# A convolution over windows of three token quarters, and copies that two engines share, in a fused convolution and wave-MLP kernel

## The chip, the cores and the metric

The kernel runs on one core of a Trainium2 chip. The metric is the device time of one execution in microseconds (us), the median of several runs. The engines are named as in the profile: PE is TensorE (matmul; PEld are its weight loads), DVE is VectorE, ACT is ScalarE, POOL is GpSimd, SP is SyncE. SP computes nothing; it issues DMA transfers. PSUM, where matmuls write, has eight banks.

## The reference

With x of shape 8 x 4224 x 192 (batch, tokens, channels), the reference computes a causal convolution over tokens with 7 taps, whose weights are a softmax per head (8 heads of 24 channels), and then a wave-MLP layer on its result:

```
w   = softmax(weight)                         # 8 heads x 7 taps
x   = sum_k w[h, k] * x_padded[b, s + k, h]   # 6 zero tokens ahead
theta  = x @ w_theta                          # 192 x 192
zr, zi = x * cos(theta), x * sin(theta)
y   = w_tok_r @ zr + w_tok_i @ zi             # 4224 x 4224, over tokens
u   = x + y
out = u + relu(u @ w_ch)                      # 192 x 192
```

Nearly all the arithmetic is in the two products over tokens. They have the form of a block product of two-by-two blocks.

## The kernel before

**Tiles.** Batch and channels together are 1536 columns (N), taken in two halves of 768 (HN), each worked on as two groups of 384 (PC, index g). The 4224 input tokens are 33 chunks of 128; a chunk c is not 128 neighbouring tokens but four quarters of 32, one from each fourth of the sequence (`tokens(c, a)` with a = 0 to 3). So a quarter of chunk c+1 follows directly on the same quarter of chunk c. The output tokens are units of two blocks of 128.

**A chunk's way** (class `Chunk`). POOL loads the four quarters of x, which casts them to bf16 (`load_x`, L224), into a tile `xw` of 96 partitions with two halves; in each half stand two quarters of 32 tokens with 16 history rows ahead of each. The history rows are copied from the previous chunk's tile by four DMAs on SP (`history`, L265). Convolution (`conv`, L403): for each head two matmuls of 192 columns, one per half, accumulate into a PSUM bank; the stationary operand `bands` holds the taps as a banded matrix. Two heads share a bank, so a chunk takes four banks and four copies of 384 columns on ACT to the tile `xz` (`conv_copy`, L411). From `xz` go: DMAs to a scratch in DRAM (`xs`, L298), used later as residual; a transposition into `uT`, by PE (L438) and a DVE copy (L443) for the first 11 chunks, by DMA later; the product with theta's weights (L452), copied and clamped by DVE into `ang` (L320); sine and cosine by ACT (L348); products with `xz` by DVE (L357); and three or four differences by DVE (L369), of which `t4` is the last. The product over tokens takes seven block products in place of eight, which is why the differences of blocks are needed.

**Visits.** The kernel has 11 slots for finished chunks. A visit takes one output unit and multiplies it with all chunks that lie in slots (L659); chunk c enters at visit c for the first 11 and one by one later, so the first visits are short: v+1 chunks at visit v, with 14 matmuls of 384 columns per chunk. A visit's token weights are loaded by POOL (8 DMAs, tiles `st`, L485), turned by DVE (L507) and combined by DVE (L521). Its six PSUM banks (rows x, y and s, two groups each) are added to accumulators `d`: the first sum on ACT (L684), later ones on DVE (L686); after the first product one bank is copied to another on ACT (L731). Accumulators are stored to and loaded from DRAM between visits (`part`, L698 and L621). After a unit's last visit `output` casts u to bf16 (ACT, L780), turns it (DMA, or PE for the last four visits), multiplies it with `w_ch` (L452), applies relu and adds (DVE, L799), and stores (L806).

**Order.** The program writes every engine's order out itself. All work is a list of `Step`s with an engine, a supposed duration, what must come before, and a due time; `Schedule` plays the list through with these supposed durations, first as a rehearsal, and issues the instructions of each engine in the order that results. Engines then execute in that order. Six PSUM banks belong to the visits; two (numbers 6 and 7, `mm`) are for convolution, transposition and channel products, and a step that reads such a bank frees it (`frees`). `Ring`s count the buffers of `xw`, `xz`, `uT`, `ang` and others, two of each. `START` gives the times from which engines take part, after what is issued before the list: ahead of it stand the first loads of x, the masks (POOL), the bands (DVE) and 18 matmuls on zeros (L881).

Of the kernel before, what the change touches and what calls it, by code (L numbers as in the profile page):

```python
# [10 lines left out]
ALU = mybir.AluOpType  # L11
# [5 lines left out]
def kernel(  # L17
# [32 lines left out]
    HALO = 16  # L50
    WR = Q + HALO
    NT = S // P
    HN = N // 2
# [7 lines left out]
    BY_PE = 4  # L61
    SMALL = 3
# [77 lines left out]
    def pair(u):  # L140
        return 2 * u + 1 < NT


# [22 lines left out]
    class Step:  # L166
        def __init__(self, engine, us, run, after=(), lands=0.0, wire=0.0, frees=None, mm=False):
            self.engine, self.us, self.run = engine, us, run
            self.after, self.lands, self.wire = list(after), lands, wire
            self.frees, self.mm = frees, mm  # L170
            self.due, self.want, self.fixed, self.end = None, None, None, None
            self.number = len(steps)
            steps.append(self)

# [20 lines left out]

    bands = constp.tile([2 * WR, 2 * H + 1, 2, Q], BF16, name="bands")
    nc.vector.memset(bands, 0.0)


    def channel_weights(w, name, after=()):  # L200
# [3 lines left out]
        def clear():  # L204
            made["t"] = t = wk.tile([P, 4, D], BF16, name=name, tag="wc", bufs=1)
            dve(nc.vector.memset(t[:, 1:3, :], 0.0))

        ready = [Step("dve", 0.25, clear, after)]
        for lo, hi, k, r0, r1 in ((0, P, 0, 0, P), (0, R, 1, P, D), (R, P, 2, 0, R), (0, P, 3, R, D)):
            ready.append(Step(  # L210
                "pool", 0.6, lambda lo=lo, hi=hi, k=k, r0=r0, r1=r1: pool(nc.gpsimd.dma_start(
                    out=made["t"][lo:hi, k, :], in_=w[r0:r1, :]
                )), ready[:1], lands=4.0, wire=0.3,
            ))
        return (lambda: made["t"]), ready

    xw = tiles(wk, 2, [2 * WR, 2, B, D], BF16, "xw")
    rings = {k: Ring(2) for k in ("xw", "xz", "uT", "ang", "xr", "st", "x", "y", "s")}
# [4 lines left out]
    def load_x(c, a, n, lo, t0, h, k):  # L223
        pool(nc.gpsimd.dma_start(  # L224
            out=xw[k][lo : lo + n, h, :, :],
            in_=x[:, t0 : t0 + n, :].rearrange("b s d -> s b d"),
        ))


    class Chunk:  # L230
        def __init__(self, c):
            self.c, self.early = c, c < SLOTS
            self.k, self.uses, prev = rings["xw"].take()
            self.loads = []
            for a in range(NQ):
                h, lo = a // 2, (a % 2) * WR
                t0 = tokens(c, a)
                if c or t0 == 0:
                    lo += HALO
                else:  # L240
                    t0 -= HALO
                n = (a % 2 + 1) * WR - lo
                args = (c, a, n, lo, t0, h, self.k)
                if c == 0:
                    if t0 == 0:
                        nc.vector.memset(xw[0][0:HALO, 0, :, :], 0.0)
                    load_x(*args)
                    s = Step("none", 0.0, None)
                    s.fixed = START["x0"]
                else:  # L250
                    s = Step(
                        "pool", 0.6, lambda args=args: load_x(*args), [prev],
                        lands=LAND["x"], wire=0.87,
                    )
                self.loads.append(s)
            self.uses += self.loads
            chunks[c] = self
            xwk = xw[self.k]
            self.filled = list(self.loads)
            if c:  # L260
                before = chunks[c - 1]

                def history(a):
                    h, lo = a // 2, (a % 2) * WR
                    sp(nc.sync.dma_start(  # L265
                        out=xwk[lo : lo + HALO, h, :, :],
                        in_=xw[before.k][lo + Q : lo + Q + HALO, h, :, :],
                    ))

                for a in range(NQ):  # L270
                    s = Step(
                        "sp", 0.6, lambda a=a: history(a), [before.loads, prev],
                        lands=LAND["history"], wire=0.15,
                    )
                    before.uses.append(s)
                    self.filled.append(s)
            self.uses += self.filled[NQ:]

        def prepare(self):
            c = self.c  # L280
            zk, self.xzuse, prev = rings["xz"].take()
            self.xz = xzt[zk]
            copies = []
            for hp in range(H // 2):
                m = Step("pe", 0.34, lambda b, hp=hp: self.conv(b, hp), [self.filled, bands_ready, prev], mm=True)
                self.uses.append(m)
                e = Step(
                    "act", 0.5, lambda b, hp=hp: self.conv_copy(b, hp), [m], frees=m
                )
                copies.append(e)  # L290
            self.xzuse += copies
            self.xf = self.xz[:, :, :].rearrange("p b d -> p (b d)")
            if c + 2 < NCH:
                Chunk(c + 2)
# [8 lines left out]
            for g in range(2):  # L303
# [3 lines left out]
                turned = transposed(src, uT, [copies, prev], self.early, "sp")  # L307
# [757 lines left out]
```

## Time and profile before

| | before |
|---|---|
| median of 3 runs, us | 1449.01 (1439.24 to 1450.27) |
| profiled execution, us | 1439.62 |
| its span, us | 1437.5 |
| mean granted TensorE clock | 0.997 |
| PE, DVE, ACT, POOL busy | 98%, 77%, 23%, 36% |
| matmuls: products over tokens / channel products / convolution / turns / on zeros | 7656 / 1056 / 528 / 228 / 18 |

The span reaches from the first to the last instruction; the profiled execution's own time is 2.1 us longer. In a line of the page's groups stand: line of the kernel, engine, operation, what is written and read, shape, number, then busy us in total, mean ns of one, and the engine's idle time just before these instructions with what ended it. In the timeline stand the start, the length from first start to last end, and what a stretch of equal instructions was. Matmuls overlap one another, so the mean length of one is not its cost. The chain of work that ended last is followed back from the last instruction; its shares say who set the time.

### The profile page before, as it was taken

The numbers are of one execution on the slowest core, as the hardware profiler recorded it, in microseconds if no ns is written. First come the engines' busy times: TensorE is split into PE (matmuls) and PEld (weight loads), VectorE is DVE, ScalarE is ACT, GpSimd is POOL, SyncE is SP. The second block draws the span as 40 slices with busy tenths as digits, with TensorE's granted clock in tenths as the row PEclk, the third lists the DMA queues.
The fourth block names the chain that finished last, engine by engine and source line by source line (L and its number), as shares of the span: only waits on it lengthen the run. The fifth ranks groups of instructions, "written<-read, shape, count | busy, mean of one in ns | idle before, by whom it ended". The sixth has DMA issues, their size and how long they took to land.

```text
span 1437.5 us, 24960 instructions
## 1 busy us (share of the span) xinstructions
PE 1408.2 (98%) x9486; PEld 895.5 (62%) x9486; DVE 1102.9 (77%) x1835; ACT 335.8 (23%) x582; POOL 512.2 (36%) x778
## 2 busy tenths in 40 slices
PE   6899999999999999999999999999999999999997
PEld 3666666666666666666666666666666666666665
DVE  7998764446778887886576788788887878787788
ACT  5764422122212212210000221122121212121221
POOL 7543321124234552133134445225553354311120
PEclk9999999999999999999999999999999999999999
DMA  9999883679999999998799999999995999999984
GB/s 140 252 220 209 155 162 94 122 131 238 202 222 239 237 225 229 225 210 198 183 195 193 234 252 234 220 224 217 250 253 124 204 279 257 220 229 208 254 209 154
DMA packets 341351, 298.44 MB, mean 208 GB/s; under 512 B 160784, under 2 KB 287760, under 8 KB 341232
## 3 DMA queue, kind: packets, MB, share of 16 engines
q0 software_dynamic: 171072, 97.81, 50.5%
q1 hardware_dynamic: 130160, 189.21, 42.6%
q10 hardware_dynamic: 40000, 9.84, 5.3%
q8 instruction: 74, 1.21, 0.4%
q14 instruction: 45, 0.37, 0.1%
HBM read 250.21 MB, written 106.56 MB: 248 GB/s over the span
## 4 chain that ended last, share of the span: by engine, by line
PE 90%; DMA 4%; DVE 2%; ACT 1%; issue 0%; ACTq 0%; DVEq 0%
PE bank L659 82%; PE bank L452 5%; DMA ubT<-ubT 3%; PE bank L403 3%; DMA out_dram<-d 1%; PE bank L438 1%; DVE d L799 0%; DVE d L686 0%; DVE w L521 0%; DMA xw<-xw 0%; DVE ubT L443 0%; ACT ubT L780 0%; DVE uT L443 0%; ACT bank L731 0%; DVE ang L320 0%
## 5 line engine op out<-in xcount | busy, mean ns | idle before, releaser
L659 PEld LDWEIGHTS <-w 128*128 128x128 bf16 x7572 | 736.7, 98 | 466.5 <-issue 5.1
L659 PE MATMUL bank<-t,w 128*128 128x384 bf16 x3198 | 558.4, 326 | 1.6 <-DVE w L521 1.4
L686 DVE TENSOR_TENSOR d<-bank,d 128x384 f32<-128x384 f32 x542 | 291.8, 548 | 186.0 <-PE bank L659 158.0
L659 PE MATMUL bank<-i,w 128*128 128x384 bf16 x2220 | 396.2, 326 | 1.2 <-ACT bank L731 0.6
L507 DVE STREAM_TRANSPOSE w<-st 128x640 bf16<-128x640 bf16 (+5 forms) x416 | 340.2, 846 | 67.0 <-PE bank L659 63.0
L659 PE MATMUL bank<-r,w 128*128 128x384 bf16 x2154 | 384.1, 326 | 1.4 <-DVE r L357 1.2
L485 POOL DMA_DIRECT2D st<-in_moe_w_tok_r_dram x244 | 140.2, 585 | 411.4 <-DVE w L507 354.5
L485 POOL DMA_DIRECT2D st<-in_moe_w_tok_i_dram x244 | 139.8, 583 | 145.8 <-DVE w L507 138.8
L521 DVE TENSOR_TENSOR w<-w 128x1408 bf16<-128x1408 bf16 (+10 forms) x220 | 183.2, 833 | 2.5
L631 POOL TENSOR_TENSOR d<-d,xr 128x768 f32<-128x768 f32 x62 | 105.6, 1704 | 142.1 <-DMA xr<-xs 91.8
L224 POOL DMA_DIRECT2D xw<-in_x_dram x132 | 76.8, 594 | 153.6 <-PE bank L403 128.0
L348 ACT ACTIVATE r<-ang,half_pi 128x768 bf16<-128x768 f32 x44 | 41.1, 933 | 310.3 <-DVE ang L320 310.3
L731 ACT ACTIVATE bank<-bank 128x384 f32<-128x384 f32 x116 | 54.8, 476 | 211.8 <-PE bank L659 196.7
L684 ACT ACTIVATE d<-bank 128x384 f32<-128x384 f32 x132 | 63.4, 491 | 160.4 <-PE bank L659 158.8
L411 ACT ACTIVATE xz<-bank 128x384 bf16<-128x384 f32 x132 | 60.5, 489 | 168.8 <-issue 115.4
L320 DVE TENSOR_SCALAR ang<-bank 128x384 f32<-128x384 f32 x132 | 68.5, 550 | 24.8 <-PE bank L452 24.4
L780 ACT ACTIVATE ubT<-d 128x768 bf16<-128x768 f32 x44 | 36.8, 842 | 147.1 <-DVE d L686 116.3
L799 DVE SCALAR_TENSOR_TENSOR d<-bank,d 128x384 f32<-128x384 f32 x106 | 55.3, 550 | 20.7 <-PE bank L452 20.1
L452 PEld LDWEIGHTS <-uT 128*128 128x128 bf16 x632 | 55.0, 98 | 17.0 <-issue 3.0
L403 PE MATMUL bank<-xw,bands 96*128 96x192 bf16 x528 | 60.6, 249 | 1.9 <-ACT xz L411 1.1
L452 PE MATMUL bank<-wth,uT 128*128 128x192 bf16 x528 | 58.0, 246 | 2.6 <-DVE ang L320 1.1
L403 PEld LDWEIGHTS <-bands 96*128 96x128 bf16 x528 | 47.4, 99 | 15.3 <-issue 4.0
(68 smaller groups left out, 546.3 us busy)
## 6 DMA issues: line engine op xcount, KB each, us to landing
part<-d SPq DMA_DIRECT2D x172, 384.0 KB, 4.2
d<-part SPq DMA_DIRECT2D x159, 384.0 KB, 5.5
st<-in_moe_w_tok_r_dram POOLq DMA_DIRECT2D x152, 176.0 KB, 6.5
st<-in_moe_w_tok_i_dram POOLq DMA_DIRECT2D x152, 176.0 KB, 7.4
out_dram<-d SPq DMA_DIRECT2D x53, 384.0 KB, 5.8
xs<-xz SPq DMA_DIRECT2D x132, 96.0 KB, 5.0
xr<-xs POOLq DMA_DIRECT2D x66, 192.0 KB, 6.4
xw<-in_x_dram POOLq DMA_DIRECT2D x129, 96.0 KB, 5.7
```

The lines of the kernel that those rows point to most:

```text
L224: pool(nc.gpsimd.dma_start(out=xw[k][lo : lo + n, h, :, :], in_=x[:, t0 : t0 + n, :].rearrange("b s d -> s b d"),))
L320: "dve", 0.55, lambda b, k2=k2, g=g: dve(nc.vector.tensor_scalar(out=self.ang[g][:, k2 * 2 * D : (k2 + 1) * 2 * D], in0=banks[b][:, 0 : 2 ...
L403: pe(nc.tensor.matmul(banks[b][:, hh * B * G : (hh + 1) * B * G], lhsT=bands[:, at : at + 2, :, :].rearrange("p z a m -> p (z a m)"), rhs= ...
L411: act(nc.scalar.activation(out=self.xz[:, :, hp * 2 * G : (hp + 1) * 2 * G].rearrange("p b (h g) -> p h b g", h=2), in_=banks[b][:, 0 : 2 ...
L452: pe(nc.tensor.matmul(banks[bk][:, b * D : (b + 1) * D], lhsT=tT[:, 3 * k + b + i, :], rhs=w[:, 2 * b + i, :], start=(i == 0), stop=(i == ...
L485: "pool", 0.58, lambda a=a, t0=t0, i=i, w=w: pool(nc.gpsimd.dma_start(out=st[i][a * Q : (a + 1) * Q, 0:nb, 0 : n * Q], in_=w[r0 : r0 + nb ...
L507: lambda c=c, ce=ce: dve(nc.vector.transpose(self.tile(name)[:, c:ce, :, :], st[i][:, at : at + NQ, c * Q : ce * Q].rearrange("p bt (c j) ...
L521: s = Step("dve", 0.15 + 0.069 * n, lambda: dve(nc.vector.tensor_tensor(out=flat(self.tile(name)), in0=flat(self.tile(p)), in1=flat(self.t ...
L631: a = Step("pool", 1.75, lambda: pool(nc.gpsimd.tensor_tensor(out=tile_(), in0=tile_(), in1=xrt[k], op=ALU.add)), [r, s])
L659: pe(nc.tensor.matmul(banks[bank][:, 0:PC], lhsT=self.w.block(a, c), rhs=chunks[c].operand(b, g), start=(start and c == self.lo), stop=(c ...
L684: act(nc.scalar.activation(out=o, in_=y, func=AT.Copy))
L686: dve(nc.vector.tensor_tensor(out=o, in0=y, in1=o, op=ALU.add))
```

## The change

The convolution no longer works on chunks but on windows. All quarters of all chunks in one row (chunk 0's four, chunk 1's four, and so on) are taken three at a time: 44 windows. A window's tile has 114 partitions: three times 32 tokens with their own 6 halo rows, loaded from DRAM together. So there are no copies of history, one matmul per head (`bands` has the taps of three quarters side by side and a zero block; which 128 columns are used depends on where the window's first quarter lies in its chunk), and a window's rows belong to one chunk or two. Its banks are copied in one or two pieces, each a range of partitions that starts at 0, 32, 64 or 96.

`copy_step` makes copies that may run on ACT or DVE: the planner puts a step with `also` into both engines' lists, and whichever is free first in its play takes it. That holds for the convolution copies of the first four chunks, the first sums and bank copies of the first four visits, and all copies of PE transposes.

In the beginning four banks of the first visit (2 to 5) are lent (`lent`) to the convolutions of the first two windows and to the transposes and theta products of the first chunk; two matmuls clear banks of the first visit afterwards. Windows 0 and 1 and theta's weights are loaded ahead of the list, before any token weights. The bands are made by one multiply for all taps and a tree of adds. The matmuls on zeros are 24, and their weights are zeros too, so they wait for DVE's memset and not for POOL's identity. `xw` and `xz` have three buffers each; the late tiles that took their space are split between both.

```diff
+    WQ = 3
+    ROWS = Q + KS - 1
+    WR = WQ * ROWS
...
+    EITHER, TURNED = 4, 11
...
+    def copy_step(o, i, after, us, frees=None, either=False):
+        def run(*b):
+            if s.engine == "dve":
+                dve(nc.vector.tensor_copy(out=o(), in_=i(*b)))
+            else:
+                act(nc.scalar.activation(out=o(), in_=i(*b), func=AT.Copy))
+        s = Step("act", us, run, after, frees=frees)
+        s.also = "dve" if either else None
+        return s
...
+    class Window:
+        def __init__(self):
...
+            self.k, self.uses, prev = rings["xw"].take()
+            for j in range(WQ):
+                c, a = divmod(self.m * WQ + j, NQ)
+                lo, t0, n = j * ROWS, tokens(c, a) - KS + 1, ROWS
...
+                    s = Step("pool", 0.6, load, [prev], lands=LAND["x"], wire=1.0)
+        def conv(self):
...
+                if lo % 2 and hi - lo > 1:
+                    copies.append((c, lo, lo + 1))
+                    lo += 1
+                copies.append((c, lo, hi))
+            at = -a0 % NQ
+            def conv(b, hp):
+                for hh in range(2):
+                    h = 2 * hp + hh
+                    pe(nc.tensor.matmul(
+                        banks[b][:, hh * B * G : (hh + 1) * B * G],
+                        lhsT=bands[:, h, at : at + NQ, :].rearrange("p z m -> p (z m)"),
+                        rhs=xw[self.k][0:WR, :, h * G : (h + 1) * G],
+                        start=True, stop=True,
+                    ))
...
+                m.lent = self.m < 2
...
+                        ), [m], 0.5, m, either=c < EITHER,
...
-                def history(a):
-                    h, lo = a // 2, (a % 2) * WR
-                    sp(nc.sync.dma_start(
-                        out=xwk[lo : lo + HALO, h, :, :],
-                        in_=xw[before.k][lo + Q : lo + Q + HALO, h, :, :],
-                    ))
...
-                for half in range(2):
-                    at = 2 * h + 1 - half
-                    pe(nc.tensor.matmul(
-                        banks[b][:, hh * B * G : (hh + 1) * B * G],
-                        lhsT=bands[:, at : at + 2, :, :].rearrange("p z a m -> p (z a m)"),
-                        rhs=xw[self.k][:, half, :, h * G : (h + 1) * G],
-                        start=(half == 0), stop=(half == 1),
-                    ))
...
-                turned = transposed(src, uT, [copies, prev], self.early, "sp")
+                turned = transposed(src, uT, [copies, prev], c < TURNED, "sp", lent=c == 0)
...
+                    m.lent = c == 0
...
-        e = Step("dve", 0.55, lambda b: dve(nc.vector.tensor_copy(
...
+        m.lent = lent
+        e = copy_step(
+            lambda: got(uT).rearrange("p k s -> p (k s)"),
+            lambda b: banks[b][:, :].bitcast(BF16)[:, 0 : 6 * P], [m], 0.6, m, either=True,
+        )
...
             if self.first and begins:
-                s = Step("act", 0.49, run, [after, self.start[q]])
+                s = copy_step(
+                    lambda: self.d[q]()[:, g * PC : (g + 1) * PC], lambda: banks[bank][:, 0:PC],
+                    [after, self.start[q]], 0.49, either=self.v < EITHER,
+                )
...
+                    if self.v == 0 and r != "x":
+                        prev[r, g] = [s for s in steps if s.frees is not None and s.frees.lent]
+                        if r == "y":
+                            prev[r, g] = [Step(
+                                "pe", 0.17, lambda k=rows[r, g]: pe(nc.tensor.matmul(
...
     def freed_xw():
-        return [s for u in rings["xw"].uses[-2:] for s in u]
+        return [s for r in ("xw", "xz") for u in rings[r].uses[-3:] for s in u]
...
-    START = {"x0": 8.0, "pe": 12.3, "dve": 12.3, "act": 6.3, "pool": 6.6, "sp": 2.0}
+    START = {"x": (8.0, 11.0), "pe": 11.3, "dve": 11.3, "act": 6.3, "pool": 11.2, "sp": 2.0, "wth": 15.0}
...
+    terms = spool.tile([WR, KS, H, Q], BF16, name="terms", tag="st")
     nc.vector.tensor_tensor(
+        out=terms, in0=taps[:, :, :].unsqueeze(2).to_broadcast([WR, KS, H, Q]),
...
+    n = KS
+    while n > 1:
+        k = n // 2
         nc.vector.tensor_tensor(
+            out=terms[:, 0:k], in0=terms[:, 0:k], in1=terms[:, n - k : n], op=ALU.add
         )
+        n -= k
...
-        for _ in range(3):
-            pe(nc.tensor.matmul(banks[k], lhsT=ident, rhs=noise, start=True, stop=True))
+        for _ in range(4):
+            pe(nc.tensor.matmul(banks[k], lhsT=noise[:, 0:P], rhs=noise, start=True, stop=True))
...
+                            if s.also and s.engine != e:
+                                s.engine, s.also = e, s.engine
+                            self.start(s, now)
```

## The prediction

> **What bounds the kernel now.** I read the page's busy shares first, then the chain of work that ended last, then the engines stretch by stretch, then the beginning in order of time.
>
> ```profile
> PE 1408.2 (98%) x9486; PEld 895.5 (62%) x9486; DVE 1102.9 (77%) x1835; ACT 335.8 (23%) x582; POOL 512.2 (36%) x778
> ...
> PE 90%; DMA 4%; DVE 2%; ACT 1%; issue 0%; ACTq 0%; DVEq 0%
> ...
> L403 PE MATMUL bank<-xw,bands 96*128 96x192 bf16 x528 | 60.6, 249 | 1.9 <-ACT xz L411 1.1
> ...
> L411 ACT ACTIVATE xz<-bank 128x384 bf16<-128x384 f32 x132 | 60.5, 489 | 168.8 <-issue 115.4
> ```
>
> TensorE is busy 98% of the span and is 90% of the chain, so a matmul less is time less, wherever TensorE has no idle time. The 249 ns of a convolution matmul is not its price, since matmuls overlap; the price is the distance between starts. The timeline of TensorE shows it:
>
> ```profile
> 12.24 0.82 PE L403 MATMUL bank<-xw,bands 96*128 96x192 bf16 x8
> ...
> 16.23 0.60 PE L452 MATMUL bank<-wth,uT 128*128 128x192 bf16 x3 [0.67 <-DMA wth<-in_moe_w_theta_dram]
> ...
> 18.27 0.95 PE L452 MATMUL bank<-wth,uT 128*128 128x192 bf16 x8 [0.62 <-DVE ang L320]
> 20.47 0.80 PE L659 MATMUL bank<-r,w 128*128 128x384 bf16 x2 [1.25 <-DVE r L357]
> ...
> 21.97 1.48 PE L403 MATMUL bank<-xw,bands 96*128 96x192 bf16 x8
> ```
>
> Eight matmuls in 0.82 us, the last 0.245 long: (0.82 - 0.245) / 7 = **0.082 us each**. At 21.97 the same eight take 1.48 us, 0.16 each: the clock is halved there. Now the stretches (us, then busy us and instruction count of TensorE, of its weight loads, of VectorE, ScalarE and GpSimd, granted clock, DMA share, GB/s):
>
> ```profile
> 20.00:30.00 10.00, 8.66 (x51) 5.47 (x51) 7.72 (x17) 7.42 (x16) 6.88 (x13) 0.66 1.07 138
> 30.00:40.00 10.00, 8.44 (x54) 4.40 (x52) 9.79 (x24) 8.52 (x17) 3.81 (x7) 1.00 1.19 263
> 40.00:50.00 10.00, 9.05 (x73) 6.15 (x74) 9.75 (x23) 7.71 (x17) 7.04 (x14) 1.00 1.13 227
> 50.00:60.00 10.00, 8.95 (x77) 6.25 (x76) 9.82 (x21) 7.36 (x15) 5.22 (x10) 1.00 1.27 278
> 60.00:70.00 10.00, 10.00 (x81) 6.96 (x80) 8.93 (x18) 5.67 (x12) 4.41 (x8) 1.00 1.29 264
> ...
> 400.00:428.00 28.00, 28.00 (x190) 17.91 (x189) 22.25 (x38) 5.86 (x10) 7.19 (x14) 1.00 1.02 229
> ...
> 1120.00:1200.00 80.00, 77.38 (x527) 49.50 (x526) 66.98 (x114) 17.45 (x25) 34.47 (x47) 1.00 1.14 244
> 1200.00:1300.00 100.00, 98.70 (x678) 63.72 (x677) 80.61 (x139) 17.57 (x25) 34.60 (x48) 1.00 1.22 232
> 1300.00:1400.00 100.00, 97.97 (x699) 64.35 (x698) 80.77 (x151) 20.30 (x29) 20.58 (x36) 1.00 1.15 224
> 1400.00:1438.00 38.00, 30.08 (x254) 20.78 (x251) 30.41 (x62) 7.38 (x10) 0.00 (x0) 0.98 0.47 154
> ```
>
> Three stages. Until about 60 us VectorE sets the pace (9.8 of 10 us) and ScalarE is at 7 to 8.5. From about 80 to 1120 TensorE has no gap, with VectorE at some 80%. From 1120 on TensorE loses 2.6 + 1.3 + 2.0 + 7.9 = 13.9 us to waits for turned outputs and to the drain at the end.
>
> **The change, part by part.** The sum is made against the profiled execution: 1439.6 us, a span of 1437.5 and 2.1 around it. Of the three timed runs one lies beside it (1439.2), two lie some 10 us above (1449.0, 1450.3); the median shown is such a one, 9.4 us over the profile. So a difference of about 1% is what a measurement of this kernel can tell from none.
>
> *Convolution.* Before: 33 chunks x 8 heads x 2 halves = 528 matmuls. After: 44 windows x 8 heads = 352, with the same 192 columns. 176 fewer x 0.082 = **-14.4 us**. That a contraction over 114 partitions rather than 96 costs nothing is seen from the weight loads: 99 ns with 96 rows (L403), 98 with 128 (L659).
>
> *How much of it counts.* In the paced stage it does not: by 72 us six chunks are convolved, 96 matmuls, for which eight windows need 64; 32 x 0.082 = 2.6 us that VectorE hides, of which I count **+2.3** as not gained. The 1040 us in which TensorE has no gap keep their part: VectorE has 5 to 6 us free of every 28 there.
>
> *Copies out of PSUM.* A window seldom fits one chunk: of every four windows one needs one copy per bank and three need two, so 308 copies in place of 132. A copy of 32 or 64 partitions has the same 384 columns in each, and I price it like the whole one, 0.49 us on ScalarE (L411), 0.55 on VectorE (as L320, which also reads 384 columns of PSUM). ScalarE has the room on average: 23% busy. At the beginning it may not. I counted the instructions of both kernels in their order, up to the last VectorE combination of the fourth chunk (t4; it ends at 63.0 us before). VectorE: 7 turned copies (uT) fewer, 8 copies to xz, 3 to bank, 7 to d more: 11 x 0.55 = **6.0 us more**, on 55.3 summed, which took 47.7 us of wall from 15.33 on (instructions overlap, factor 1.16), so 5.2 of wall. Against it, VectorE's first copy follows the first convolution at about 12.8 in place of 15.33. Remainder **+2.5**; bounds: 0, if all of it fills the waits of 20 to 30 us (2.3 idle), and +5.2, if the early start gains nothing. ScalarE up to the same chunk: 16 xz x 0.49, 6 uT x 0.84 (as L780), less 3 bank and 6 d x 0.49 = +8.5, on 37.5 in 45 us: dense, not over.
>
> *First steps.* Bands: seven multiplies of 256 columns and six adds become one of 1792 (2.4 to 2.9, seven times 0.34 to 0.42), adds of 768, 512 and 256 columns (0.55 + 0.41 + 0.29), two mask sums (0.86) and three products of 512 (0.84 to 1.68, from 0.28 for 256): 5.4 to 6.7 against 6.0 from masks to bands. The masks end 0.1 to 0.9 later, as they are half as wide again and one load of x stands before them. So bands at -0.5 to +1.5. Against that, theta's weights are asked for before the token weights, which takes away the waits of 0.67 and 0.25 us for them, and four lent banks the wait of 0.62 for ang. The token weights pass to the back of GpSimd's queue, behind 6 loads of x and 4 of theta (0.57 to 0.66 each in before's list): their last lands near 18.5, and the second pair is first turned near 20. Together **0** (-1.5 to +1.5). The two clearing matmuls of the first visit: 2 x 0.16 = +0.3.
>
> *Warm-up.* Eighteen matmuls from 6.75 to 12.4 become 24 that wait only for a memset ending at 1.78, so they end near 9, and TensorE idles some 3 us before the first convolution. The row: after the thin stretch from 12.4 to 20.5 the clock is halved from 20.5 to 27 (0.66 in that line). If the pause halves it earlier, 16 convolutions, 12 turns and 16 mixes of the first chunk take 3.3 us longer, part of it beside copies; I take 0 and keep 3.3 for the range. [...]
>
> *History transfers.* 128 DMAs leave SyncE's queue, and with them a hop in front of each convolution. TensorE waited 0.43 us for one at 21.7, and the chain goes through one for 3.94 us at 52.13, where TensorE then lost 1.2: at best -1.7, taken as 0. x's rows grow from 32 to 38: 132 x 6 x 8 = 6336 more packets on q0, at 50.5% x 16 x 1437.5 / 171072 = 68 ns each, 27 us of each engine's time, 2% of the span; history's 6.3 of q1's 189.2 MB at 42.6% are 1.4% back. Even; and GpSimd's queue waits for VectorE (493 us before token weights), not for DMA.
>
> *End.* Six of thirteen turned copies go to ScalarE (0.84 for 0.55, but beside VectorE), the late buffers wait for two rings, not one: -2 to +4, taken as 0.
>
> Sum: 1437.5 - 14.4 + 2.3 + 2.5 + 0.3 = 1428.2; with 2.1 around it **1430.3**, 0.65% less.
>
> **The rivals.** *The beginning gains too* (chance 0.30): the added copies fill VectorE's waits, the early part of the 14.4 is kept, the first product comes 1.5 us sooner and the drain gains 1.5. 1437.5 - 14.4 + 0.3 - 3.0 + 2.1 = 1422.5. For it: VectorE waits 3.19 us for its first turned copy; against it: 9.8 of 10 from 30 to 60.
>
> *Given back at the end* (0.09): the buffers of the extra visits come later, and half of the 13.9 us of late waits is added: 1437. For it: these visits' weights need both rings free; against it: conv ends near 1056, a long way before.
>
> *ScalarE's queue becomes the bound* (0.11), the slower side. Up to the last sine of the eleventh chunk it gets 52 more copies to xz, 15 uT, 3 bank and 7 d fewer: 20.6 + 12.6 = +33 us on 108 in 173 us of wall. It issues in order, so a copy that waits for its matmul holds up the sines and the d copies behind it, and these hold TensorE. If nothing hides them: 1437.5 - 14.4 + 0.3 + 33.2 + 2.1 = 1459. It decides against the change from 14 of the 33 us on. Against it: ScalarE idles 1.5 to 4 us of every 10 here, and two copies in a row start 0.39 us apart, not 0.49.
>
> **How the numbers follow.** Forecast 0.50, its own range 1423 to 1439; a fifth of that lies below 1425.2, the 1% mark. Faster by over 1%: 0.10 + 0.30 = 0.40; within: 0.40 + 0.09 = 0.49; slower: 0.11. The range takes in the first two rivals, and the forecast with the upper group of runs, 1440; the last rival's 0.11 is left out: 1417 to 1445.
>
> **What would show it.** 352 convolution matmuls 0.082 us apart, and no gaps from 100 to 1100: right for the main term. First product near 20 us, VectorE again at 9.7 of 10 until 60, t4 of the fourth chunk near 65: right for the early terms. TensorE's share below 97% with ScalarE as releaser before 200 us: the slower rival. Wrong altogether if token weights come too late for the second visit, or if DMA, at a share over 1 in most stretches, keeps the shorter visits waiting.

## The result

The changed kernel is slower: a median of **1596.04 us** (1591.87 to 1616.18) against 1444.59 us of the kernel before on the same chip (1439.24 to 1450.27), a ratio of **1.104** (95% interval 1.097 to 1.111). Forecast was 1430.3 us. The profiled execution took 1596.84 us, a span of 1595.0, 157.5 more than before. A run more than 1.5% above the fastest of its kernel (here the one of 1616.18) stands in the medians and not in the ratios, and every ratio is against the kernel before on the same chip.

On the page of the changed kernel, the lines that answer to those shown of before: the engines' busy time, the queue of GpSimd's transfers (packets, MB, share of 16 engines' span), the chain that ended last, two groups, and x's loads (number, KB each, median us from issue to landing).

```profile
PE 1442.9 (90%) x9318; PEld 900.5 (56%) x9318; DVE 1085.3 (68%) x1823; ACT 429.5 (27%) x763; POOL 623.6 (39%) x782
...
q0 software_dynamic: 455744, 101.19, 60.6%
...
DMA 29%; PE 27%; issue 7%; POOL 6%; DVE 4%; SPq 1%; ACTq 0%; ACT 0%; DVEq 0%; POOLq 0%
...
L267 POOL DMA_DIRECT2D xw<-in_x_dram x132 | 189.2, 1441 | 69.7 <-PE bank L304 29.5
...
L304 PE MATMUL bank<-xw,bands 114*128 114x192 bf16 x352 | 54.9, 256 | 20.6 <-DMA xw<-in_x_dram 8.7
...
xw<-in_x_dram POOLq DMA_DIRECT2D x131, 114.0 KB, 13.7
```

The same queue and the same loads of before:

```profile
q0 software_dynamic: 171072, 97.81, 50.5%
...
L224 POOL DMA_DIRECT2D xw<-in_x_dram x132 | 76.8, 594 | 153.6 <-PE bank L403 128.0
...
xw<-in_x_dram POOLq DMA_DIRECT2D x129, 96.0 KB, 5.7
```

TensorE falls from 98% to 90%, and of the chain from 90% to 27%; DMA rises from 4% to 29%. To issue a transfer of x takes GpSimd 1.44 us; before it was 0.59. And q0 has 455,744 packets where before it had 171,072, with 3.4 MB more. The prediction counted 6336 more. That number is the thread to pull.

The waits of the changed kernel (engine, line, what it waited for: us in all, times, longest):

```profile
POOL st L523 <- DMA xw<-in_x_dram: 193.1, 75, 8.0
...
DVE w L545 <- DMA st<-in_moe_w_tok_r_dram: 115.0, 20, 16.0
...
DVE w L545 <- DMA st<-in_moe_w_tok_i_dram: 88.0, 28, 9.5
```

In the kernel before, the same three come to 3.4 us in all (the wait for `st<-in_moe_w_tok_r_dram` is not in its list):

```profile
DVE w L507 <- DMA st<-in_moe_w_tok_i_dram: 3.0, 3, 1.5
...
POOL st L485 <- DMA xw<-in_x_dram: 0.4, 1, 0.4
```

GpSimd, about to ask for token weights, waits 193 us for earlier loads of x; VectorE then waits 203 us for token weights that come late, and TensorE some 100 us for VectorE (40.2 for sums, 35.2 for theta's angles, 20.4 for turned token weights, 7.0 for turned copies). The stretches (us, then busy us and instruction count of TensorE, its weight loads, VectorE, ScalarE, GpSimd, clock, DMA share, GB/s) say where, first of before, then of after:

```profile
0.00:80.00 80.00, 64.10 (x459) 40.58 (x460) 68.48 (x157) 49.40 (x96) 51.25 (x102) 0.96 1.11 197
80.00:1120.00 1040.00, 1039.93 (x6880) 656.62 (x6878) 775.67 (x1217) 223.72 (x397) 371.29 (x546) 1.00 0.95 204
```

```profile
0.00:80.00 80.00, 44.41 (x226) 25.15 (x227) 45.45 (x104) 36.79 (x68) 53.45 (x78) 0.72 1.01 102
80.00:1120.00 1040.00, 947.10 (x6012) 585.50 (x6010) 673.58 (x1080) 289.13 (x540) 409.33 (x486) 0.96 1.08 179
```

Half the matmuls are missing by 80 us (226 for 459), and the middle stretch, gapless before, has 93 us of gaps. GpSimd's queue in order of time, of the changed kernel, shows how it begins:

```profile
22.37 8.58 POOL L267 DMA_DIRECT2D xw<-in_x_dram  x6
30.94 1.73 POOL L523 DMA_DIRECT2D st<-in_moe_w_tok_r_dram  x3
33.99 0.58 POOL L523 DMA_DIRECT2D st<-in_moe_w_tok_r_dram  x1 [1.32 <-DMA xw<-in_x_dram]
```

Six loads of x hold the queue for 8.58 us; the six land at 31.8 to 43.9, and the four transfers of token weights behind them land 44.2 to 45.0, the first of them 13.3 us after its issue. Before, four loads of x took 2.28 us there. The wait of 1.32 us is of another kind: the program gives GpSimd's transfers eight semaphores in turn (102 to 109 in the trace), so each waits until the one eight places ahead has landed. Counted over the trace, 143 of GpSimd's 694 transfers start within 0.6 us of that landing, 34 before; in the first 200 us, 6.5 of the eight places are taken on average, 3.9 before.

**Theory S (shape).** The trace's DMA records point to the reason. Each of the 131 loads of 38 rows brings 304 packets of data (38 rows, 8 batches) and, beyond the 16 four-byte packets that every transfer has (11,104 for the 694 of before), 2128 more of four bytes (fillers): 131 x 2128 = 278,768. The remaining 5,904 of the 284,672 that q0 has more are rows of data. 2128 is 14 x 152, and 152 is half of 304. The counts fit data on 2 of 16 engines, 152 rows each, and as many fillers on each of the other 14; the trace does not name the engine of a packet. It does show how many are under way at once: before, up to 29 packets of 384 bytes with one load of 32 rows alone (issued at 22.82 us); in the changed kernel, from 22.4 to 44 us, with up to six loads of 38 rows, never more than 11. Theory S supposes that a load is spread over as many engines as the largest number up to 16 that divides its rows: 2 for 38, and 16 for the former 32 and 48, whose loads have no fillers. Three numbers of rows do not show that; the runs below test it. With hardly anything ahead of it such a load lands after 8.6 us (152 packets of 56 ns are 8.5); before, 3.1 to 4.2.

### The profile page after: what moved, and what is told of

The parts are those of the page before. It is cut to its first block, busy times and chain, and to the rows that moved or that the text cites. A ratio compares the mean times of both kernels' runs of the same rounds, so it can differ in the third digit from the quotient of the medians.

```text
span 1595.0 us, 24505 instructions
## 1 busy us (share of the span) xinstructions
PE 1442.9 (90%) x9318; PEld 900.5 (56%) x9318; DVE 1085.3 (68%) x1823; ACT 429.5 (27%) x763; POOL 623.6 (39%) x782
## 3 DMA queue, kind: packets, MB, share of 16 engines
q0 software_dynamic: 455744, 101.19, 60.6%
## 4 chain that ended last, share of the span: by engine, by line
DMA 29%; PE 27%; issue 7%; POOL 6%; DVE 4%; SPq 1%; ACTq 0%; ACT 0%; DVEq 0%; POOLq 0%
PE bank L702 24%; DMA st<-in_moe_w_tok_r_dram 10%; DMA st<-in_moe_w_tok_i_dram 7%; DMA xw<-in_x_dram 6%; POOL xw L267 3%; PE bank L490 2%; POOL d L674 2%; DVE w L545 2%; DMA ubT<-ubT 2%; DVE d L726 1%; DMA uT<-ub 1%; DMA part<-d 1%; POOL st L523 1%; DMA d<-part 1%; DMA out_dram<-late 1%
## 5 line engine op out<-in xcount | busy, mean ns | idle before, releaser
L702 PEld LDWEIGHTS <-w 128*128 128x128 bf16 x7572 | 744.8, 99 | 540.8 <-issue 72.8
L702 PE MATMUL bank<-t,w 128*128 128x384 bf16 x3198 | 564.1, 328 | 9.0 <-DVE d L726 8.2
L702 PE MATMUL bank<-r,w 128*128 128x384 bf16 x2154 | 408.7, 334 | 28.7 <-DVE w L545 19.6
L702 PE MATMUL bank<-i,w 128*128 128x384 bf16 x2220 | 402.7, 332 | 27.3 <-DVE d L726 24.2
L267 POOL DMA_DIRECT2D xw<-in_x_dram x132 | 189.2, 1441 | 69.7 <-PE bank L304 29.5
L185 ACT ACTIVATE xz<-bank 64x384 bf16<-64x384 f32 (+2 forms) x300 | 139.9, 481 | 144.9 <-issue 75.2
L490 PE MATMUL bank<-wth,uT 128*128 128x192 bf16 x528 | 67.5, 272 | 47.5 <-DVE ang L378 35.2
L490 PEld LDWEIGHTS <-uT 128*128 128x128 bf16 x632 | 61.3, 107 | 74.1 <-issue 40.6
L378 DVE TENSOR_SCALAR ang<-bank 128x384 f32<-128x384 f32 x132 | 70.2, 551 | 30.8 <-PE bank L490 30.2
L304 PE MATMUL bank<-xw,bands 114*128 114x192 bf16 x352 | 54.9, 256 | 20.6 <-DMA xw<-in_x_dram 8.7
L304 PEld LDWEIGHTS <-bands 114*128 114x128 bf16 x352 | 34.7, 102 | 41.0 <-issue 15.6
## 6 DMA issues: line engine op xcount, KB each, us to landing
st<-in_moe_w_tok_r_dram POOLq DMA_DIRECT2D x152, 176.0 KB, 10.4
st<-in_moe_w_tok_i_dram POOLq DMA_DIRECT2D x152, 176.0 KB, 10.8
xw<-in_x_dram POOLq DMA_DIRECT2D x131, 114.0 KB, 13.7
```

The lines of the kernel that those rows point to most:

```text
L185: act(nc.scalar.activation(out=o(), in_=i(*b), func=AT.Copy))
L267: pool(nc.gpsimd.dma_start(out=xw[self.k][lo : lo + n, :, :], in_=x[:, t0 : t0 + n, :].rearrange("b s d -> s b d"),))
L304: pe(nc.tensor.matmul(banks[b][:, hh * B * G : (hh + 1) * B * G], lhsT=bands[:, h, at : at + NQ, :].rearrange("p z m -> p (z m)"), rhs=xw[ ...
L378: "dve", 0.55, lambda b, k2=k2, g=g: dve(nc.vector.tensor_scalar(out=self.ang[g][:, k2 * 2 * D : (k2 + 1) * 2 * D], in0=banks[b][:, 0 : 2 ...
L490: pe(nc.tensor.matmul(banks[bk][:, b * D : (b + 1) * D], lhsT=tT[:, 3 * k + b + i, :], rhs=w[:, 2 * b + i, :], start=(i == 0), stop=(i == ...
L702: pe(nc.tensor.matmul(banks[bank][:, 0:PC], lhsT=self.w.block(a, c), rhs=chunks[c].operand(b, g), start=(start and c == self.lo), stop=(c ...
```

## Is it the shape?

**One number changed: 42 and 40 rows per load.** More halo rows than are used (42 is 3 x 14, 40 is 4 x 10), so more bytes, and the same matmuls.

```diff
-    ROWS = Q + KS - 1
+    ROWS = 42        # in the other run 40
+    HALO = ROWS - Q
...
-                lo, t0, n = j * ROWS, tokens(c, a) - KS + 1, ROWS
+                lo, t0, n = j * ROWS, tokens(c, a) - HALO, ROWS
...
```

> The changed kernel with one number altered: a quarter's load has 42 rows instead of 38 (10 halo rows instead of 6; a window has 126 partitions; the four added rows meet zeros in the bands). Theory S (shape of the transfer): a load of 38 rows runs on only 2 of the 16 DMA engines, since 2 is the largest number up to 16 that divides 38, and the other 14 get fillers of 4 bytes (14 x 152 = 2128, which is the surplus found per load); 42 rows run on 14 engines. Then about 48 fillers per load in place of 2128, queue q0 at about 190,000 packets in place of 455,744, issue back to 0.6 us from 1.44, landing 4 to 7 us in place of 13.7, and the time 1420 to 1440. Theory B (bytes and rows read from DRAM hold it up): 10% more of them, so 1600 or more. Theory C (308 copies saturate ScalarE and VectorE) and theory W (three loads per window, shared by two chunks, come too late by the dependencies): unchanged, 1590 to 1600.

> The changed kernel with loads of 40 rows. Theory S: 40 is divided by 10, so 10 engines with 32 rows-by-batch each and 6 x 32 = 192 fillers per load; landing between those of 42 rows and of 38 and much nearer to 42's, 1425 to 1450. If instead only powers of two divided the work, it would be 8 engines and 320 fillers. Theories B, C, W: 1590 to 1605.

Measured: 42 rows 1451.5 us, ratio 1.0052 (1.0028 to 1.0075); 40 rows 1430.7, 0.992 (0.989 to 0.994), two runs only. 42 rows lie a little above the range given for theory S, 40 rows within it.

```profile
q0 software_dynamic: 187456, 101.71, 53.2%
...
xw<-in_x_dram POOLq DMA_DIRECT2D x131, 126.0 KB, 5.2
```

```profile
q0 software_dynamic: 204224, 100.98, 52.7%
...
xw<-in_x_dram POOLq DMA_DIRECT2D x131, 120.0 KB, 5.7
```

Fillers are 131 x 48 and 131 x 192, as theory S gives with 14 and 10 engines; x is issued in 0.68 and 0.73 us. Nearly all of the 150 us is gone with the shape.

**The kernel before, with halo rows loaded directly:** 38 rows in place of 32 and the copies, then 48.

```diff
...
-                if c or t0 == 0:
+                if t0 == 0:
...
+                elif c:
+                    lo += HALO - 6       # in the other run 16
+                    t0 -= 6
...
-            if c:
-                before = chunks[c - 1]
-                def history(a):
...
```

> The kernel before, its convolution, copies and planner untouched, but each quarter after the first chunk is loaded with 6 halo rows from DRAM in one DMA of 38 rows, and the history copies are left out. Theory S: the shape alone brings the loss, about 2128 fillers per load, issue 1.44 us, 1540 to 1600. Theories C and W: 1435 to 1445, since neither windows nor added copies are there. Theory B: a little over before, 1445 to 1460.

> As the run before it, but with all 16 history rows, one DMA of 48 rows per quarter: half as many bytes again as 32 rows. Theory S: 48 is divided by 16, no fillers, issue 0.6 us; 1435 to 1450. Theory B: slower than the run with 38 rows, over 1460.

Measured: 38 rows 1608.7 us, ratio 1.115 (1.112 to 1.118), a little over the range of theory S, with 128 x 2128 fillers; 48 rows 1446.8, 1.003 (1.000 to 1.006), with none. So neither windows nor shared copies nor lent banks are needed for the loss, and half as many rows again cost next to nothing.

**41 and 39 rows, and 38 in two transfers.** The last is the changed kernel's own rows, cut where the sizes divide well (its planner counts 1.2 us in place of 0.6 for the two issues):

```diff
-                    pool(nc.gpsimd.dma_start(
-                        out=xw[self.k][lo : lo + n, :, :],
-                        in_=x[:, t0 : t0 + n, :].rearrange("b s d -> s b d"),
-                    ))
+                    for r0, r1 in ((0, n - Q), (n - Q, n)):
+                        if r1 > r0:
+                            pool(nc.gpsimd.dma_start(
+                                out=xw[self.k][lo + r0 : lo + r1, :, :],
+                                in_=x[:, t0 + r0 : t0 + r1, :].rearrange("b s d -> s b d"),
+                            ))
...
-                    s = Step("pool", 0.6, load, [prev], lands=LAND["x"], wire=1.0)
+                    s = Step("pool", 1.2, load, [prev], lands=LAND["x"], wire=1.0)
```

> The changed kernel with 41 rows per load (9 rows of halo, of which the last 6 are used). 41 is divisible by no number from 2 to 16, so theory S (shape) has the load on one engine and 15 x 41 x 8 = 4920 fillers of 4 bytes per load, 131 x 4920 = 644,520 surplus packets on q0. Two theories on how that costs time: (serial) the loads of one queue land one after the other, and a load lasts as long as its longest engine: 328 rows x 56 ns = 18.4 us, so 131 loads need at least 2406 us, and the kernel takes 2400 to 2600 us. (issue) what costs is GpSimd's time for writing the descriptors: 5248 packets against 2432 with 38 rows, so some 3.1 us per load in place of 1.44, 217 us more of GpSimd, which by the run with small GpSimd instructions is worth 37 / 118.6 of that, some 70 us: about 1670 us, and at most 1596 + 217 = 1813. A rival to both: one row more brings nothing new, and it is again near 1430 or 1596.

> The changed kernel with 39 rows per load, one more than it has and two fewer than the run beside it. 39 = 3 x 13: 13 engines, 3 x 24 = 72 fillers, 131 x 72 = 9432 surplus packets. Theory S: as with 40 and 42 rows, 1430 to 1450 us, x's loads land in 5 to 6 us and are issued in 0.6 to 0.7 us. If the number of rows mattered by bytes or in any smooth way, it would lie between the 38 and the 40 rows, above 1500.

> The changed kernel with the same 38 rows, but each loaded by two transfers, 6 rows of halo (6 engines, 10 x 8 = 80 fillers) and 32 rows (16 engines, none). 132 more transfers of GpSimd. Theory S: most of the loss goes although rows, bytes and matmuls are those of the changed kernel; 1430 to 1455 us, the 132 further issues of 0.6 us being 79 us of GpSimd, worth up to 25 us by the run with small GpSimd instructions. Theory of bytes or of packets of data: no gain, 1590 or more.

Measured: 41 rows **2065.9 us** (ratio 1.432, 1.423 to 1.441), 39 rows 1448.4 (1.002, 0.999 to 1.005), 38 as 6 + 32 rows 1442.0 (1.000, 0.997 to 1.003). One row more or less than 40 decides over 600 us in one direction and next to nothing in the other. Of the 41-row kernel, the queue, the group of x's loads, and their KB and median landing:

```profile
q0 software_dynamic: 824640, 103.86, 60.0%
...
L268 POOL DMA_DIRECT2D xw<-in_x_dram x132 | 328.8, 2496 | 277.5 <-issue 192.6
...
xw<-in_x_dram POOLq DMA_DIRECT2D x131, 123.0 KB, 20.1
```

Of the kernel with 38 rows in two parts:

```profile
q0 software_dynamic: 189552, 100.13, 53.0%
...
L269 POOL DMA_DIRECT2D xw<-in_x_dram x263 | 151.1, 582 | 166.8 <-PE bank L306 100.2
...
xw<-in_x_dram POOLq DMA_DIRECT2D x132, 96.0 KB, 4.7
xw<-in_x_dram POOLq DMA_DIRECT2D x131, 18.0 KB, 4.3
```

Theory S holds in its counts: fillers are 131 x 4920 with 41 rows, 131 x 80 with 6 + 32, and 131 more issues of 0.58 us cost nothing that is seen. But both prices that I had put on the 41 rows missed. Loads do not follow one another (2406 us): the first took 14.8 us with hardly anything ahead of it, but those issued back to back landed 6.0 us apart in the median (3.2 to 11.7; with 38 rows 2.7, from 0.7 to 8.6). They overlap. And GpSimd's issue time alone (1670) is far too little.

The 41-row kernel has a wait of its own. GpSimd stands for a long time where the profile names no releaser:

```profile
POOL xw L268 <- issue: 192.6, 54, 13.2
POOL st L524 <- issue: 188.8, 34, 11.4
```

The landings tell what ends most of it. Of its 96 such waits before transfers, 385 us in all, 62 with 363 us end 0.31 to 0.43 us after a load of x has landed, with one or two more loads of x still under way. Never are more than three under way, against six with 38 rows. Why GpSimd stands there was not shown.

## How does the shape cost time?

**Told to the planner.** Is it only that the order was planned with loads issued in 0.6 us that land early? The changed kernel, with x at 1.44 us, landing after 13 (early in the plan too, where other landings count half), and later start times:

```diff
-                    s = Step("pool", 0.6, load, [prev], lands=LAND["x"], wire=1.0)
+                    s = Step("pool", 1.44, load, [prev], lands=LAND["x"], wire=1.0)
...
-        "x": 9.0, "keep": 6.0, "turn": 11.0, "w": 8.0, "d": 7.5, "store": 5.5,
+        "x": 13.0, "keep": 6.0, "turn": 11.0, "w": 8.0, "d": 7.5, "store": 5.5,
...
```

> The changed kernel with loads of 38 rows as they are, but its planner is told what the trace shows of them: 1.44 us to issue, 13 us to land, first windows at 13.4 and 19.2 us, engines' start times moved accordingly. Theory L (lateness: the loads are only later than the plan supposes, and everything behind them in GpSimd's order is placed for the old times): the plan asks for them earlier and most of the loss after 80 us goes, 1450 to 1500. Theory T (throughput: slow landings hold GpSimd's in-order queue, since each of its DMAs waits for the one eight places ahead of it, and no order helps): 1560 to 1600.

Measured: 1591.0 us, ratio 1.103 (1.099 to 1.108); GpSimd still waits 178.5 us before token weights for x. A plan that knows the price does not avoid it.

**GpSimd's time alone.** 40 rows, and after each load from the third window on nine small memsets on GpSimd:

```diff
+                    for _ in range(9 if self.m > 1 else 0):
+                        pool(nc.gpsimd.memset(idle, 0.0))
```

> Loads of 40 rows, and after each load from the third window on nine small memsets on GpSimd (0.6 to 1.1 us together, about the 0.72 to 0.86 us by which a load of 38 rows takes longer to issue). Takes the issue time by itself, without the fillers and the late landing. If the 112 us of added issue time on GpSimd make the loss: 1520 to 1600. If landing makes it (POOL is busy 37% and waits 480 us for VectorE anyway): 1428 to 1445.

Measured: 1467.3 us, ratio 1.0175 (1.013 to 1.022); the memsets were busy for 118.6 us in all. Neither range was met. Against 40 rows without them (1430.7 by the two runs then at hand, 1438.5 by the twelve below), 29 to 37 us. The changed kernel's loads hold GpSimd for 189.2 - 76.8 = 112 us more than before, so by this run GpSimd's time alone makes some 30 us of about 150.

**The same kind of transfer, with data that nobody waits for.** 40 rows, and behind each load from the third window on a transfer of 38 rows of two elements:

```diff
+                    if self.m > 1:
+                        spare = dram.tile([38, B + 1, 4], BF16, name=f"spare{self.m}_{lo}")
+                        pool(nc.gpsimd.dma_start(
+                            out=spare[:, 0:B, 0:2], in_=x[:, t0 : t0 + 38, 0:2].rearrange("b s d -> s b d"),
+                        ))
```

> The 40-row version; from the third window on, each load of x is followed by a further transfer on GpSimd's queue, of 38 rows of two elements each, from x to a place in DRAM that nothing reads (304 packets of data on two engines, 2128 fillers on the others). The load of x itself stays in the good shape, ahead of it. If the loss of the changed kernel comes from the transfers around x (GpSimd's issue, the eight places, token weights behind in the queue), all of it comes back, and more, as there are 126 further transfers: 1580 to 1750 us, GpSimd's token weights waiting for earlier transfers as in the changed kernel (193 us). If it comes from x's own late landing, only GpSimd's time counts: 126 x 1.44 = 181 us of it, by the run with small GpSimd instructions 37 / 118.6 each, 57 us: about 1490.

Measured: 1740.4 us, ratio 1.207 (1.199 to 1.215). Its page's table of transfers and its waits:

```profile
xw<-in_x_dram POOLq DMA_DIRECT2D x131, 120.0 KB, 11.0
spare<-in_x_dram POOLq DMA_DIRECT2D x126, 1.2 KB, 13.4
```

```profile
DVE w L551 <- DMA st<-in_moe_w_tok_r_dram: 211.4, 24, 25.9
...
POOL st L529 <- DMA spare<-in_x_dram: 168.7, 58, 8.0
...
DVE w L551 <- DMA st<-in_moe_w_tok_i_dram: 103.8, 21, 22.2
```

A transfer of 1.2 KB takes 13.4 us, and 126 of them add 300 us, without one of them being used. 131 further transfers with 80 fillers each (6 + 32 rows) cost nothing, so it is not their number. The same waits stand here as in the changed kernel, on another name. One thing came out otherwise than built: x itself landed after 11.0 us and not after 5.7 as in the first run with 40 rows, with the spare transfers among its loads in the queue, so this run alone does not rule out that convolution waits for its data. The lists of waits speak against it: TensorE waits for x only once, 13.1 us here and 8.7 in the changed kernel.

So the loss is made around x's loads, by a queue that fills: long transfers (13.7 us in the median in the changed kernel), eight at most under way, and what stands behind lands late (token weights of 176 KB after 10.4 and 10.8 us, before 6.5 and 7.4). How much of the 150 us falls to the eight places and how much to lateness in the queue is not separated; taking either away alone was not tried. Nor is a third part: the four-byte packets of q0 take 221 us of each engine's time in the mean in the changed kernel against 13 before, and SyncE's transfers on another queue land later too (accumulators stored in 6.6 us for 4.2, xz in 7.7 for 5.0).

## Do the other terms hold once the shape is right?

**40 rows again, with more runs.**

> The 40-row version once more, with more runs. If the first two runs were typical, 1428 to 1433 us and a ratio of 0.990 to 0.993, as the forecast had it (0.9935 of its own profile). If they were lucky in the last stage, where other rows and variants with the same early part lost up to 25 us more, the median lies at 1434 to 1440 us, a ratio of 0.994 to 0.998.

Measured: 1438.5 us (1428.7 to 1452.0, before 1441.6), ratio **0.9973** (0.9946 to 1.0001), which is not told from no change. The first two runs were lucky, and the three experiments below, whose ranges were set against their 1430, started from a wrong base. The stretches of its profiled execution (1437.0 us), in the same columns as above:

```profile
0.00:80.00 80.00, 63.84 (x396) 37.62 (x397) 68.46 (x151) 58.12 (x107) 56.09 (x104) 0.89 1.13 179
80.00:1120.00 1040.00, 1040.00 (x6824) 652.17 (x6822) 788.80 (x1231) 302.53 (x560) 391.84 (x556) 1.00 0.98 204
1120.00:1436.00 316.00, 298.56 (x2102) 195.16 (x2100) 247.62 (x442) 67.98 (x97) 86.15 (x124) 0.98 1.08 216
```

The middle has no gap. I summed, for each stretch, by how much TensorE's starts lie further apart than a matmul's length at full clock. Up to 80 us: 30.8 us lost and a start at 1.4, in place of 20.0 and 6.75, so 5.4 more. After 1120: 19.2 in place of 14.3, 4.9 more. Convolution has 14.4 less work, the matmuls on zeros and the clearing ones 1.6 more. Together -14.4 + 1.6 + 5.4 + 4.9 = -2.5; the spans differ by 2.3.

One place at the end accounts for the 4.9 and more. TensorE in order of time, 40 rows:

```profile
1202.01 0.83 PE L491 MATMUL bank<-wch,ubT 128*128 128x192 bf16 x8 [1.95 <-DMA ubT<-ubT]
1202.68 1.46 PE L703 MATMUL bank<-i,w 128*128 128x384 bf16 x8
1209.62 1.46 PE L491 MATMUL bank<-wch,uT 128*128 128x192 bf16 x8 [5.47 <-DMA uT<-ub]
1210.88 1.49 PE L703 MATMUL bank<-i,w 128*128 128x384 bf16 x4
```

A turned output asked for at 1189.5 lands after 20.1 us, TensorE waits 5.47 us for it, and the eight matmuls behind the pause take 1.46 us, where those at 1202.01 took 0.83. In the kernel before, the turned output of that moment (1196.3) took 6.6 us. Next to it in the changed order are four loads of token weights and two of accumulators within some 3 us, all landing after 11 to 19 us. But in the kernel before such loads stand as near (four of token weights from 1197.0 on, one of accumulators at 1193.8) and land after 6 to 8 us, so meeting them does not explain it by itself. In the first run with 40 rows the same output took 14.9 us, the wait was 2.30, and the eight matmuls behind it took 0.83. Why it lands late stays open.

**More matmuls on zeros, up to the first convolution** (36 for 24), with 40 rows:

```diff
-        for _ in range(4):
+        for _ in range(6):
             pe(nc.tensor.matmul(banks[k], lhsT=noise[:, 0:P], rhs=noise, start=True, stop=True))
```

> Loads of 40 rows, and 36 matmuls on zeros in place of 24, so that they last until about 11.6 us, when the bands are ready, and not until 9.0. If the pause of 2.7 us halves the clock (convolution at 0.16 to 0.19 us per matmul in the run with 40 rows, granted clock 0.75 between 20 and 40 us, TensorE 12 us short there against 8 before): full clock until after the first chunk, 2 to 5 us less, 1426 to 1429. If the thin work of 12 to 25 us halves it anyway: within 1 us of the run with 40 rows, 1430.

Measured: 1435.9 us, ratio 0.9957 (0.9932 to 0.9983). Neither range was met, as both were set against 1430. TensorE's pause before the first convolution falls from 2.71 to 0.87 us. The first convolutions, 40 rows with 24 (its first profile, then its second), then with 36:

```profile
11.71 0.83 PE L305 MATMUL bank<-xw,bands 120*128 120x192 bf16 x8 [2.71 <-DVE bands L935]
12.70 1.37 PE L305 MATMUL bank<-xw,bands 120*128 120x192 bf16 x8 [0.15 <-DVE xz L184]
```

```profile
11.73 2.13 PE L305 MATMUL bank<-xw,bands 120*128 120x192 bf16 x16 [2.47 <-DVE bands L935]
```

```profile
11.71 1.94 PE L305 MATMUL bank<-xw,bands 120*128 120x192 bf16 x16 [0.87 <-DVE bands L935]
```

In the first profile the second eight run at half clock from the third on (1.37 us in all, the first eight 0.83). In the second, after nearly the same pause, the clock falls only at 13.33 us and all but the last two of the sixteen start at the distance of full clock; with 36 it falls at 14.70. So the pause did not decide over the second eight, and the clock falls within the next stretch of work in all three (granted clock 0.66 to 0.67 from 10 to 20 us and again from 20 to 30 with 24; 0.83 and 0.58 with 36). The time agrees with that of 24 within both intervals.

**Copies not shared, and no lent banks**, each with 40 rows:

```diff
-    EITHER, TURNED = 4, 11
+    EITHER, TURNED = 0, 11
...
-        e = copy_step(
-            lambda: got(uT).rearrange("p k s -> p (k s)"),
-            lambda b: banks[b][:, :].bitcast(BF16)[:, 0 : 6 * P], [m], 0.6, m, either=True,
-        )
+        e = Step("dve", 0.55, lambda b: dve(nc.vector.tensor_copy(
...
```

```diff
-                m.lent = self.m < 2
+                m.lent = False
...
-                    if self.v == 0 and r != "x":
+                    if False:
```

> Loads of 40 rows, and no copy may change engine: convolution copies, first sums and bank copies on ScalarE, turned copies on VectorE, as before. By the prediction's count VectorE gets 11 instructions less up to the fourth chunk (6 us summed) and ScalarE 18 copies more there. If VectorE still paces the beginning: 0 to 3 us faster than 1430. If sharing fills waits: 3 to 10 us slower.

> The 40-row version without lent PSUM banks and without the two clearing matmuls; the sharing of copies stays. If lending is what lets the first chunk's transposes and theta products pass without waiting, the first product starts 0.6 to 2 us later and the whole takes 1432 to 1437 us; if VectorE's pace until 60 us decides, as the prediction has it, the difference is under 1 us: 1430 to 1432.

Measured: not shared 1441.7 us, 0.9990 (0.9966 to 1.0013); not lent 1439.9, 0.9975 (0.9945 to 1.0005). TensorE's loss up to 80 us is 36.6 and 32.6 us in their profiles, for 30.8 with both; the two profiles of 40 rows differ there by 1.0. So in these profiles sharing gains some 5 to 6 us at the beginning, where I had counted the added copies as a loss, and lending 2 at most; the whole times do not show either.

## Why the prediction was wrong

- *History transfers* failed, and it alone turned the sign. "x's rows grow from 32 to 38: 132 x 6 x 8 = 6336 more packets on q0, at ... 68 ns each" counted the added rows only, and called the balance "Even". It was 284,672 more packets, issue 1.44 for 0.59 us, landing 13.7 for 5.7. The trace of before, with 32 and 48 rows only and no fillers, could not show what 38 rows bring. Its second half failed with it: "GpSimd's queue waits for VectorE (493 us before token weights), not for DMA" was right of before and false 193 us long of after. Taken as 0, the step was worth about +155 us (1596.0 against 1438.5 with 40 rows).
- That token weights come too late, or DMA "keeps the shorter visits waiting", was named as the way to be wrong altogether, without a price or a chance, and so the range did not reach it. Late token weights are what came. None of the three rivals did: ScalarE is at 27%, and TensorE's waits for it come to some 4 us.
- *Convolution*, -14.4: 352 matmuls, eight in 0.83 us, as forecast, and the sum over the 40-row profile closes with it.
- *How much of it counts* and *Copies out of PSUM*, +4.8 with the clearing's 0.3 beside: with the shape put right 5.4 + 1.6 = 7.0, where the 1.6 holds the clearing and six more matmuls on zeros. The sum came near; its parts did not, since sharing made up for part of what copies cost.
- *First steps*, 0: the first product starts at 20.34 us in the 40-row kernel, 20.47 before. Right.
- *Warm-up*, 0 with 3.3 kept: the clock falls earlier than before (12.80 and 13.33 us in the two profiles of 40 rows, 20.25 before), and with the pause mostly removed still at 14.70; removing it moved no time that could be told.
- *End*, 0 (-2 to +4): +4.9 in the 40-row kernel, not for buffers but mostly for one turned output that lands later.

With the shape right the forecast of -9.3 us would have met about -3: right in sign, and within what a measurement of this kernel hardly tells from none. Of the versions run, 40 rows with 36 matmuls on zeros is the only one with ten runs whose interval lies below 1: 0.4% under the kernel before. It is not told from 40 rows with 24, and one of so many versions may come out so by chance.

## What to carry to other kernels

Before a transfer's first size is changed, factor it: what counted here is the largest divisor up to 16 of the number of rows, not the bytes; 39, 40, 42 or 6 + 32 rows (13, 10, 14, 6 and 16) ran at 0.997 to 1.005 of the time before, 38 (2) at 1.104 and 41 (1) at 1.432. When a queue is said to wait for an engine, ask how long its transfers may get before it waits for itself: with eight places and 13.7 us in the median for a load of x, it did so 75 times, 193 us in all. And count packets first: one line of the page, q0 with 455,744 for 171,072 at almost equal MB, points to the whole case.

## What the runs showed of the hardware

- Beyond the 16 four-byte packets of every transfer, a load of x has 2128 with 38 rows, 4920 with 41, 192 with 40, 48 with 42, none with 32 or 48. As an estimate from these counts, a load's packets of data are spread over as many of 16 engines as the largest divisor of its rows up to 16, and each other engine gets as many four-byte packets as one of these gets of data. With 38 and 41 rows each took 12 ns in the mean, and GpSimd's issue grows with their number: 0.59 us (32 rows) and 0.64 (48) with none, 0.68 with 48, 0.73 with 192, 1.44 with 2128, 2.50 with 4920.
- Loads of 38 and 41 rows overlap: the first lands after 8.6 us (38 rows) and 14.8 (41), those issued back to back land 2.7 and 6.0 us apart in the median.
- With 41 rows GpSimd stands 381 us before loads of x and token weights for nothing that the profile names; of its 385 us of such waits before transfers, 363 end just after a load of x has landed. With 38 rows it stands 10.4 us before token weights.
- The last stage varies between versions with the same early part: losses after 1120 us of 11 to 36 us in the profiles of 39, 40 and 42 rows (14.3 before), of which TensorE's waits for turned outputs are 3.0 to 14.6 us (5.5 before). The slowest turned output took 16 to 20 us there, and 16 before.
